# One block of linear attention and a Mish MLP: kv by squares of 64 channels, z in two float32r parts, and a reordered first block

## The chip, the cores and the metric

One core of one Trainium2 chip. The metric is the device time of one execution in microseconds; lower is better. The core has a matmul engine (TensorE, "PE" in the profile; its weight loads are the row "PEld"), VectorE ("DVE"), ScalarE ("ACT"), GpSimd ("POOL") and a queue engine that issues transfers ("SP").

## What is computed

The reference, cut to what matters here. x has 2048 rows of 512 channels; there are 32 heads of 16 channels.

```python
mod = (_silu(c) @ w_mod).reshape(c.shape[0], 6, 1, -1)
sa, ca, ga, sb, cb, gb = (mod[:, i] for i in range(6))

h = _layernorm(x) * (1 + ca) + sa
q, k, v = split_heads(h @ wqkv)                       # 32 heads of 16 channels
phi = lambda t: jnp.where(t > 0, t + 1, jnp.exp(t)) + 1e-6
pq, pk = phi(q), phi(k)
kv  = jnp.einsum("bhsd,bhse->bhde", pk, v)            # 16 x 16 per head
z   = jnp.einsum("bhsd->bhd", pk)
num = jnp.einsum("bhqd,bhde->bhqe", pq, kv)
den = jnp.einsum("bhqd,bhd->bhq", pq, z)[..., None] + 1e-6
x = x + ga * ((num / den) merged @ wo)

h = _layernorm(x) * (1 + cb) + sb
x = x + gb * (mish(h @ w1 + b1) @ w2)                 # 512 -> 1792 -> 512
```

## The kernel before

**Precision.** PE multiplies fp32 operands in two instructions per matmul. Most products instead use operands split in two float32r parts, a high part `h` (a rounding copy) and a low part `l` (the rest), and three matmuls `h*h + h*l + l*h`: that is `mm3` (lines 67 to 69), and `split` (lines 71 to 81) makes the parts, with the copy at L75 (ACT) or L77 (another engine) and the subtraction at L80. A few small products stay in plain fp32: the sums z (L277), their spreading zbc (L476), kv (L738), the products of kv and wo (L748) and the denominators (L591).

**Order.** The kernel is written under a manual schedule: on each engine, instructions run in the order in which the Python code issues them. Work that should lie between PE's units is written as generators; `spawn` adds one, and each `tick` lets every running generator issue its next piece. So moving a line moves its instructions in the queue of its engine. SBUF holds a pool of 101 tiles of 128 x 512, and PSUM has four accumulators ("acc"), three "h" banks and one "tp" bank.

**Stages.** The 2048 rows are four blocks of four tiles of 128 rows.

1. First block (lines 345 to 447). The statistics of the four tiles of x are taken, and `apply` (L339) normalises them, on ACT (L195, which needs a shift computed on DVE, L190) or on DVE (L197). `mod_col` (L162) makes the columns of the modulation: column 0 (shift) and column 4 (scale) are needed first; `plus_one` (L166) adds one. PE transposes the tiles (L371) into `tp0[k]`; ACT writes `hT_x_0_k` as its high half `hi`, and then the full value back in place (both L393); DVE subtracts for the low half (L405). PE then runs the k projections in rounds over the four tiles: high by high (L412), then high by low and low by high (L415).
2. For blocks 0 to 3: `k_unit`, phi of k, and `g_unit`, which adds products of phi(k) with the normalised x to `gacc`. `make_constants` (L140) fills the masks on POOL between the second and the third unit of block 0; right behind it POOL makes the high halves of block 1 (`transpose(..., pool)`, L455), which DVE (L80) and PE need.
3. `z_unit` (L273) sums phi(k) over the rows by four matmuls into four strips of 32 partitions, and ACT copies the result to `zsum`. `z_side` (L473) multiplies it by `w32`, a matrix of 1/32, which adds up the strips on all partitions; ACT copies it to `zbc_sb`, and DVE makes from it the scaled head masks (`hmask`) and `zs`.
4. The q projections (`q_unit`). Between them: `attend` (L586) makes the denominators `den` with stationary operands of 32 columns, four strips side by side (L591); kv is made of 16 matmuls, group g of 128 channels by k (L738), of which only the 16 x 16 squares of the heads are kept by a product with `bmask` (L740); and `m_ps` (L748) multiplies kv by the scaled wo.
5. `o_unit`, the second normalisation, and the MLP by two-by-two blocks with seven products each (`product`, `pair_unit`, `d_unit`).

These are the lines of kv that the change replaces:

```python
    kv_ps = ps("acc", "kv_ps")
    for g in range(4):
        cs = slice(P * g, P * (g + 1))
        for k in range(4):
            pe.matmul(kv_ps[:, cs], wv[k][:, cs], zs[k][:, cs], start=k == 0, stop=k == 3)
```

Of the kernel before, what the change touches and what calls it, by code (L numbers as in the profile page):

```python
# [8 lines left out]
F32 = mybir.dt.float32  # L9
F32R = mybir.dt.float32r  # L10
AF = mybir.ActivationFunctionType
ALU = mybir.AluOpType

P = 128
# [11 lines left out]
def block_kernel(ctx: ExitStack, tc: tile.TileContext, x, wqkv, wo, w1, b1t, w2, c, wmodt, out):  # L26
    nc = tc.nc
    act, dve, pool, pe, sp = nc.scalar, nc.vector, nc.gpsimd, nc.tensor, nc.sync

    cst = ctx.enter_context(tc.tile_pool(name="cst", bufs=1))  # L30
# [7 lines left out]
    def sb(name, dt=F32, shape=(P, 512)):  # L38

        return big.tile(list(shape), dt, tag="T", name=name, bufs=SLOTS)  # L40

    def ps(tag, name, shape=(P, 512)):
        return psp.tile(list(shape), F32, tag=tag, name=name, bufs=PBUFS[tag])

    def f32(t):
        return t.bitcast(F32)
# [14 lines left out]
    def run(gen):  # L61
        for _ in gen:
            pass
# [7 lines left out]
    def split(name, t, keep, key, lo_engine=dve, hi_engine=act):  # L71

        hi, lo = sb(f"{name}h", F32R, t.shape), sb(f"{name}l", F32R, t.shape)
        if hi_engine is act:
            act.activation(hi, t, AF.Copy)  # L75
        else:
            hi_engine.tensor_copy(hi, t)  # L77
        if lo_engine is dve:
            yield
        lo_engine.tensor_tensor(lo, t, f32(hi), op=ALU.subtract)  # L80
        keep[key] = hi, lo


    xt, wm, wraw = {}, {}, {}
# [46 lines left out]
    sc_bc = ps("acc", "sc_bc")  # L131
# [1 line left out]
    warm_up(3)  # L133
    ident = cst.tile([P, P], F32, name="ident")
    make_identity(nc, ident)
    w32 = cst.tile([P, P], F32, name="w32")
    bmask = cst.tile([P, P], F32, name="bmask")
    hmask = cst.tile([P, 4, 32], F32, name="hmask")

    def make_constants():  # L140
        pool.memset(w32, 1.0 / 32)

        pool.memset(bmask, 1.0)
        bm3 = bmask.rearrange("p (a r) -> p a r", r=16)
        pool.affine_select(bm3, bm3, pattern=[[-16, 8], [0, 16]], compare_op=ALU.is_ge,
                           fill=0.0, base=0, channel_multiplier=1)
        pool.affine_select(bm3, bm3, pattern=[[16, 8], [0, 16]], compare_op=ALU.is_ge,
                           fill=0.0, base=15, channel_multiplier=-1)

        pool.memset(hmask, 1.0)  # L150
        pool.affine_select(hmask, hmask, pattern=[[128, 4], [-16, 32]], compare_op=ALU.is_ge,
                           fill=0.0, base=0, channel_multiplier=1)
        pool.affine_select(hmask, hmask, pattern=[[-128, 4], [16, 32]], compare_op=ALU.is_ge,
                           fill=0.0, base=15, channel_multiplier=-1)


    mc = cst.tile([P, 24], F32, name="mc")
    sc_row = sb("sc_row")

    def mod_col(i, row):  # L160
        t = wm.pop(i)
        dve.scalar_tensor_tensor(t, t, 1.0, row, op0=ALU.mult, op1=ALU.mult,  # L162
                                 accum_out=mc[:, i:i + 1])

    def plus_one(lo, hi):
        dve.tensor_scalar(mc[:, lo:hi], mc[:, lo:hi], 1.0, 1.0, op0=ALU.add, op1=ALU.mult)  # L166
# [16 lines left out]
    def ln_rstd(key, b, lo=0, hi=4):  # L183

        y = rs[key, b][:, lo:hi]
        pool.tensor_tensor(y, y, half[:, lo:hi], op=ALU.pow)  # L186

    def ln_shift(key, b, lo=0, hi=4):

        dve.scalar_tensor_tensor(nb[key, b][:, lo:hi], mv[key, b][:, lo:hi, 0], -1.0, rs[key, b][:, lo:hi],  # L190
                                 op0=ALU.mult, op1=ALU.mult)

    def ln_apply(key, b, j, t, dst, engine):
        if engine is act:
            act.activation(dst, t, AF.Identity, bias=nb[key, b][:, j:j + 1], scale=rs[key, b][:, j:j + 1])  # L195
        else:
            engine.tensor_scalar(dst, t, mv[key, b][:, j, 0:1], rs[key, b][:, j:j + 1],  # L197
                                 op0=ALU.subtract, op1=ALU.mult)
# [16 lines left out]
    def sums_shift(key, b, t, sums):  # L215
        dve.tensor_tensor(nb[key, b][:, t:t + 1], sums[:, 0:1], rs[key, b][:, t:t + 1], op=ALU.mult)  # L216

    xn, hT, wq, wk = {}, {}, {}, {}
# [49 lines left out]
            cs = slice(P * k, P * (k + 1))  # L268
            mm3(gacc[k], [h[:, cs] for h in xn[b, t]], pk[b, t], b == 0 and t == 0, b == NB - 1 and t == 3)

    zsum = sb("zsum")

    def z_unit():  # L273

        p = ps("h", "z")
        for t in range(4):
            pe.matmul(p[32 * t:32 * (t + 1), :], ones[:, 0:32], ku.pop((0, t)), start=True, stop=True)  # L277
        act.activation(zsum, p, AF.Copy)

    def q_unit(b, g):  # L280
        p = ps("h", f"pq_{b}_{g}")
# [57 lines left out]
    def apply(b, t, engine, shift=True):  # L339
        v = xt["x", b, t]  # L340
        if engine is act and shift:
            ln_shift("x", b, t, t + 1)
        ln_apply("x", b, t, v, v, engine)

    tp0 = [ps("acc", f"tp_x_0_{k}") for k in range(3)]
# [5 lines left out]
    sums_eps("x", 0, 2, sums)  # L351
    ln_eps("x", 0, 3, 4)
    ln_rstd("x", 0, 3, 4)
    wk_0 = split("wk_0", wraw[1, 0], wk, 0)
    next(wk_0)
    apply(0, 1, dve)
    sums_shift("x", 0, 2, sums)
    apply(0, 2, act, shift=False)
    mod_col(4, sc_bc)
    plus_one(4, 5)  # L360
    apply(0, 3, dve)
    mod_col(0, sc_bc)
    run(wk_0)

    def transposes_0(k, p):
        for t in range(4):
            pe.transpose(p[:, P * t:P * (t + 1)], xt["x", 0, t][:, P * k:P * (k + 1)], ident)
# [6 lines left out]
    def mod_pair(k):  # L374
        mod_col(4 + k, sc_bc)
        plus_one(4 + k, 5 + k)
        mod_col(k, sc_bc)
# [6 lines left out]
    def step(*gens):  # L384
        for g in gens:
            next(g, None)

    tss = [slice(P * t, P * (t + 1)) for t in range(4)]
    for k in range(4):
        hi, lo = sb(f"hT_x_0_{k}h", F32R), sb(f"hT_x_0_{k}l", F32R)  # L390
        hT["x", 0, k] = hi, lo
        for dst in (hi, tp0[k]):
            act.activation(dst, tp0[k], AF.Identity, bias=mc[:, k:k + 1], scale=mc[:, 4 + k:5 + k])  # L393
        if k < 3:
            run(split(f"wk_{k + 1}", wraw[1, k + 1], wk, k + 1, pool, pool))
        if k == 0:
            act.preload_act_table_set("exp_and_others")
            mod_pair(1)
        if k == 1:
            step(xsplit[0])  # L400
            mod_col(7, sc_bc)
            plus_one(7, 8)
        if k == 3:
            step(xsplit[0])
        dve.tensor_tensor(lo, tp0[k], f32(hi), op=ALU.subtract)  # L405
        if k == 0:
            mod_pair(2)
        if k == 1:
            mod_col(3, sc_bc)
        if k < 2:  # L410
            for t in range(4):
                pe.matmul(kp[t], hi[:, tss[t]], wk[k][0], start=k == 0, stop=False)  # L412
            for st, mv_ in (hi, wk[k][1]), (lo, wk[k][0]):
                for t in range(4):
                    pe.matmul(kp[t], st[:, tss[t]], mv_, start=False, stop=False)  # L415
        if k == 0:
            tp0.append(ps("acc", "tp_x_0_3"))
            transposes_0(3, tp0[3])
# [27 lines left out]
    apply(1, 3, act, shift=False)  # L446
    step(xsplit[3], kpost[3])
    make_constants()
    for j in range(4):
        load_x(2, j)  # L450
# [11 lines left out]
    wv, wos = {}, {}  # L462
# [8 lines left out]
    zs = {}  # L471

    def z_side():  # L473

        zbc_ps = ps("tp", "zbc")
        pe.matmul(zbc_ps, w32, zsum, start=True, stop=True)  # L476
        zbc = sb("zbc_sb")
        act.activation(zbc, zbc_ps, AF.Copy)
        yield
        for g in range(4):  # L480
            diag = cst.tile([P, P], F32, tag="diag", name=f"diag_{g}", bufs=1)
            dve.scalar_tensor_tensor(diag, zbc[:, P * g:P * (g + 1)], 1.0, ident, op0=ALU.mult, op1=ALU.mult,
                                     accum_out=zc[:, g:g + 1])
            dve.tensor_scalar(hmask[:, g, :], hmask[:, g, :], zc[:, g:g + 1], 1.0, op0=ALU.mult, op1=ALU.mult)
        for k in range(4):
            zs[k] = sb(f"zs_{k}")
            dve.tensor_scalar(zs[k], zbc, mc[:, k:k + 1], 1.0, op0=ALU.mult, op1=ALU.mult)
# [245 lines left out]
    spawn(attending)  # L733
    kv_ps = ps("acc", "kv_ps")
    for g in range(4):
        cs = slice(P * g, P * (g + 1))
        for k in range(4):
            pe.matmul(kv_ps[:, cs], wv[k][:, cs], zs[k][:, cs], start=k == 0, stop=k == 3)  # L738
    kv = sb("kv")
    dve.tensor_tensor(kv.rearrange("p (g m) -> p g m", g=4), kv_ps.rearrange("p (g m) -> p g m", g=4),  # L740
                      bmask.unsqueeze(1).to_broadcast([P, 4, P]), op=ALU.mult)
    for g in range(1, 4):
        q_unit(1, g)
        load_x(2, g, "r")
# [230 lines left out]
```

## Time and profile before

| what | us |
|---|---|
| median of 3 runs (506.63 to 507.06) | 506.66 |
| the profiled execution | 506.48 |
| its span | 504.8 |
| PE busy | 497.4 |
| DVE busy | 359.7 |
| ACT busy | 256.7 |
| POOL busy | 113.0 |

The span runs from the first to the last instruction of the profile; the 1.7 us between span and time lie around it. "Busy" is the time in which an engine had an instruction under way. Matmuls are pipelined, so a row's duration is longer than its distance from the next: a float32r matmul of 512 columns has a row of 0.39 us, and the next begins 0.23 us later. The chain of waits gives each instruction its share of the time instead, and is the view to take costs of PE from. In the timelines a row reads: start and duration in us, engine, line, operation, output and inputs, shapes, count, and in brackets how long the engine had been idle and what released it.

### The profile page before, as it was taken

The numbers are of one execution on the slowest core, as the hardware profiler recorded it, in microseconds if no ns is written. First come the engines' busy times: TensorE is split into PE (matmuls) and PEld (weight loads), VectorE is DVE, ScalarE is ACT, GpSimd is POOL, SyncE is SP. The second block draws the span as 40 slices with busy tenths as digits, with TensorE's granted clock in tenths as the row PEclk, the third lists the DMA queues.
The fourth block names the chain that finished last, engine by engine and source line by source line (L and its number), as shares of the span: only waits on it lengthen the run. The fifth ranks groups of instructions, "written<-read, shape, count | busy, mean of one in ns | idle before, by whom it ended". The sixth has DMA issues, their size and how long they took to land.

```text
span 504.8 us, 6832 instructions
## 1 busy us (share of the span) xinstructions
PE 497.4 (99%) x2364; PEld 407.8 (81%) x2364; DVE 359.7 (71%) x705; ACT 256.7 (51%) x461; POOL 113.0 (22%) x203
## 2 busy tenths in 40 slices
PE   7999999999999999999999999999999999999996
PEld 6778888878778888878888888888888888888885
DVE  6889785878997969986987785359886556745302
ACT  6767573523351987736677765357253344445000
POOL 4480000100212411210233345421210111470000
PEclk9999999999999999999999999999999999999999
DMA  8721504561543315372566599983842445596102
GB/s 311 274 83 44 166 21 126 167 209 49 139 132 92 88 36 178 104 227 66 156 199 186 144 295 264 347 237 92 242 135 63 125 126 163 137 354 223 41 0 83
DMA packets 52232, 77.28 MB, mean 153 GB/s; under 512 B 5805, under 2 KB 20277, under 8 KB 52198
## 3 DMA queue, kind: packets, MB, share of 16 engines
q0 software_dynamic: 19600, 37.45, 25.6%
q1 hardware_dynamic: 32452, 39.14, 24.8%
q8 instruction: 18, 0.29, 0.2%
q10 hardware_dynamic: 146, 0.26, 0.1%
q14 instruction: 16, 0.13, 0.1%
HBM read 60.83 MB, written 15.99 MB: 152 GB/s over the span
## 4 chain that ended last, share of the span: by engine, by line
PE 88%; DVE 7%; DMA 2%; ACT 1%; POOL 1%; issue 0%; SPq 0%; DVEq 0%; ACTq 0%
PE oacc L68 10%; PE oacc L69 10%; PE oacc L67 10%; PE p_s L67 5%; PE p_s L69 5%; PE p_s L68 5%; PE p_a L68 3%; PE p_a L69 3%; PE p_a L67 3%; PE pq L67 3%; PE pq L68 3%; PE pq L69 3%; PE gacc L68 3%; PE gacc L69 3%; PE gacc L67 3%; PE pk L69 2%
## 5 line engine op out<-in xcount | busy, mean ns | idle before, releaser
L509 POOL DMA_DIRECT2D w2b<-w2d x84 | 44.9, 538 | 102.6 <-PE p_a L69 27.3
L817 ACT ACTIVATE ub<-c,b1c 128x512 f32<-128x512 f32 x28 | 19.1, 719 | 57.2 <-DVE c L826 53.5
L826 DVE TENSOR_TENSOR u<-p_s,u 128x512 f32<-128x512 f32 x28 | 19.3, 691 | 35.2 <-PE p_s L69 25.5
L809 DVE TENSOR_TENSOR rb<-oacc,rb 128x512 f32<-128x512 f32 x8 | 5.5, 692 | 32.9 <-PE oacc L69 32.9
L826 DVE TENSOR_TENSOR u<-p_a,u 128x512 f32<-128x512 f32 x26 | 17.6, 688 | 7.5 <-PE p_a L69 6.9
L691 ACT ACTIVATE hf_n<-tp_n,mc 128x512 f32<-128x512 f32 x16 | 11.7, 772 | 21.1 <-PE tp_n L689 21.1
L186 POOL TENSOR_TENSOR rs_n<-rs_n,half 128x1 f32<-128x1 f32 x16 | 9.4, 589 | 54.1 <-DVE rs_n L212 44.4
L238 ACT ACTIVATE e_q<-pq 128x512 f32<-128x512 f32 x16 | 9.4, 589 | 21.5 <-PE pq L69 21.5
L794 ACT ACTIVATE u<-u,b1c 128x512 f32<-128x512 f32 x26 | 18.5, 713 | 2.6 <-DVE u L826 2.6
L826 DVE TENSOR_TENSOR c<-p_s,u 128x512 f32<-128x512 f32 x28 | 17.9, 683 | 1.9 <-PE p_s L69 1.9
L843 ACT ACTIVATE u<-p_a 128x512 f32<-128x512 f32 x12 | 7.1, 588 | 18.7 <-PE p_a L69 18.7
L238 ACT ACTIVATE e_k<-pk 128x512 f32<-128x512 f32 x16 | 9.4, 591 | 13.4 <-PE pk L69 13.3
L186 POOL TENSOR_TENSOR rs_x<-rs_x,half 128x1 f32<-128x1 f32 (+1 forms) x10 | 7.1, 718 | 32.9 <-DVE rs_x L181 32.1
L240 DVE TENSOR_SCALAR e_k<-e_k 128x512 f32<-128x512 f32 x16 | 6.8, 423 | 10.4 <-ACT e_k L238 10.2
L195 ACT ACTIVATE x<-x,nb_x,rs_x 128x512 f32<-128x512 f32 x14 | 10.8, 806 | 4.3 <-DVE nb_x L190 3.3
L598 POOL DMA_DIRECT2D rden_d<-rden x3 | 2.2, 739 | 47.9 <-DVE rden L596 47.9
L610 DVE TENSOR_TENSOR q<-q,rd 128x512 f32<-128x512 f32 x16 | 10.5, 686 | 2.6 <-DMA rd<-rden_d 2.6
L622 DVE TENSOR_TENSOR r<-o,r 128x512 f32<-128x512 f32 x16 | 10.8, 681 | 1.7 <-PE o L69 1.6
L195 ACT ACTIVATE r<-r,nb_n,rs_n 128x512 f32<-128x512 f32 x8 | 6.5, 808 | 10.1 <-DVE nb_n L216 9.3
L241 DVE SCALAR_TENSOR_TENSOR ku<-pk,e_k 128x512 f32<-128x512 f32 x16 | 11.1, 692 | 0.8
L241 DVE SCALAR_TENSOR_TENSOR q<-pq,e_q 128x512 f32<-128x512 f32 x16 | 11.1, 691 | 0.8
L177 DVE BATCH_NORM_STATS2 st_x<-x 128x6 f32<-128x512 f32 x13 | 8.9, 682 | 3.1 <-DMA x<-in_x_dram 3.1
(1116 smaller groups left out, 1757.0 us busy)
## 6 DMA issues: line engine op xcount, KB each, us to landing
w2b<-w2d POOLq DMA_DIRECT2D x84, 256.0 KB, 4.9
w1p<-in_w_dram SPq DMA_DIRECT2D x28, 256.0 KB, 3.1
wm<-in_wmodt_dram SPq DMA_DIRECT2D x24, 256.0 KB, 5.1
r<-in_x_dram SPq DMA_DIRECT2D x16, 256.0 KB, 2.6
x<-in_x_dram SPq DMA_DIRECT2D x15, 256.0 KB, 5.3
w2r<-in_w_dram SPq DMA_DIRECT2D x14, 256.0 KB, 3.4
rd<-rden_d POOLq DMA_DIRECT2D x12, 256.0 KB, 5.3
wr<-in_wqkv_dram SPq DMA_DIRECT2D x8, 256.0 KB, 3.0
```

The lines of the kernel that those rows point to most:

```text
L67: pe.matmul(o, st[0], mv[0], start=start, stop=False)
L68: pe.matmul(o, st[0], mv[1], start=False, stop=False)
L69: pe.matmul(o, st[1], mv[0], start=False, stop=stop)
L186: pool.tensor_tensor(y, y, half[:, lo:hi], op=ALU.pow)
L195: act.activation(dst, t, AF.Identity, bias=nb[key, b][:, j:j + 1], scale=rs[key, b][:, j:j + 1])
L238: act.activation(e, p, AF.Exp)
L241: dve.scalar_tensor_tensor(dst, p, 0.0, e, op0=ALU.max, op1=ALU.add)
L509: pool.dma_start(w2s[f][i], w2d[f, i])
L691: act.activation(hf[b, j], p, AF.Identity, bias=mc[:, 12 + j:13 + j], scale=mc[:, 16 + j:17 + j])
L794: act.activation(u, p, AF.Mish, bias=b1c[:, f:f + 1])
L817: act.activation(u, p, AF.Mish, bias=b1c[:, f:f + 1])
L826: dve.tensor_tensor(out, p, u, op=ALU.add)
```

## The change

- `z_unit` keeps the sums as two float32r parts, `zsum[0]` (copied by ACT) and `zsum[1]` (the rest, subtracted by DVE); `z_side` multiplies `w32`, now float32r as well, by both in turn.
- kv is made by squares of 64 by 64 channels: in each group of 128, two matmuls, one to PSUM partitions 0 to 63 and one to 64 to 127, with 64 stationary and 64 moving columns each. Two masked copies on 64 partitions replace the one on 128. What they leave out of the kv tile is zeroed beforehand: the tile is taken at the start and POOL zeroes it in `make_constants`.
- In the first block ACT, not DVE, normalises tile 1. The column products 4 and their `plus_one` come before the shift of tile 2, and the split of the first k weights, `wk_0`, comes behind column 0, in one go.
- The high half of `hT_x_0_0` is written by ACT in two pieces of 256 columns.

```diff
-    w32 = cst.tile([P, P], F32, name="w32")
+    w32 = cst.tile([P, P], F32R, name="w32")
...
+    kv = sb("kv")
+
     def make_constants():
-        pool.memset(w32, 1.0 / 32)
+        pool.memset(f32(w32), 1.0 / 32)
+        pool.memset(kv, 0.0)
...
-    zsum = sb("zsum")
+    zsum = [sb(f"zsum_{i}", F32R) for i in range(2)]
...
-        act.activation(zsum, p, AF.Copy)
+        act.activation(zsum[0], p, AF.Copy)
+        dve.tensor_tensor(zsum[1], p, f32(zsum[0]), op=ALU.subtract)
...
-    wk_0 = split("wk_0", wraw[1, 0], wk, 0)
-    next(wk_0)
-    apply(0, 1, dve)
+    apply(0, 1, act)
+    mod_col(4, sc_bc)
+    plus_one(4, 5)
     sums_shift("x", 0, 2, sums)
     apply(0, 2, act, shift=False)
-    mod_col(4, sc_bc)
-    plus_one(4, 5)
     apply(0, 3, dve)
     mod_col(0, sc_bc)
+    wk_0 = split("wk_0", wraw[1, 0], wk, 0)
     run(wk_0)
...
-        for dst in (hi, tp0[k]):
-            act.activation(dst, tp0[k], AF.Identity, bias=mc[:, k:k + 1], scale=mc[:, 4 + k:5 + k])
+
+        for dst, piece in [(hi, half_) for half_ in ((0, 256), (256, 512))] + [(tp0[k], (0, 512))] if k == 0 else \
+                [(hi, (0, 512)), (tp0[k], (0, 512))]:
+            cs = slice(*piece)
+            act.activation(dst[:, cs], tp0[k][:, cs], AF.Identity, bias=mc[:, k:k + 1], scale=mc[:, 4 + k:5 + k])
...
-        pe.matmul(zbc_ps, w32, zsum, start=True, stop=True)
+        for i in range(2):
+            pe.matmul(zbc_ps, w32, zsum[i], start=i == 0, stop=i == 1)
...
     for g in range(4):
-        cs = slice(P * g, P * (g + 1))
         for k in range(4):
-            pe.matmul(kv_ps[:, cs], wv[k][:, cs], zs[k][:, cs], start=k == 0, stop=k == 3)
-    kv = sb("kv")
-    dve.tensor_tensor(kv.rearrange("p (g m) -> p g m", g=4), kv_ps.rearrange("p (g m) -> p g m", g=4),
-                      bmask.unsqueeze(1).to_broadcast([P, 4, P]), op=ALU.mult)
+            for j in range(2):
+                cs = slice(P * g + 64 * j, P * g + 64 * (j + 1))
+                pe.matmul(kv_ps[64 * j:64 * (j + 1), cs], wv[k][:, cs], zs[k][:, cs], start=k == 0, stop=k == 3)
+    for j in range(2):
+        js = slice(64 * j, 64 * (j + 1))
+        dve.tensor_tensor(kv.rearrange("p (g m) -> p g m", g=4)[js, :, js],
+                          kv_ps.rearrange("p (g m) -> p g m", g=4)[js, :, js],
+                          bmask[js, js].unsqueeze(1).to_broadcast([64, 4, 64]), op=ALU.mult)
```

## The prediction

> **What bounds the kernel now.** I read the page first, then the list of what TensorE (PE) waited for, then the chain of waits in order of time, and last the timelines of the engines around each edit. The page says who is busy and who ends the chain:
>
> ```profile
> PE 497.4 (99%) x2364; PEld 407.8 (81%) x2364; DVE 359.7 (71%) x705; ACT 256.7 (51%) x461; POOL 113.0 (22%) x203
> ...
> PE 88%; DVE 7%; DMA 2%; ACT 1%; POOL 1%; issue 0%; SPq 0%; DVEq 0%; ACTq 0%
> ```
>
> PE is busy for 99% of the span, and 88% of the chain that ended last lies on it. The list of PE's own waits is the second half of that statement:
>
> ```profile
> PE pk L412 <- ACT hT_x_0h L393: 0.7, 1, 0.7
> ...
> PE gacc L68 <- DVE rs_x L212: 0.2, 1, 0.2
> ```
>
> The first is the largest wait for data that an edit here touches, and the rows between and after it are shorter ones. After the first block PE simply works through its instructions in order. So a microsecond less of PE work, anywhere behind the first block, should come off the end, unless another engine then becomes late; and a microsecond of delay on DVE, ACT or POOL costs nothing until it reaches PE. The chain in order of time shows the PE stretches that the change shortens (start, length in us, what):
>
> ```profile
> 107.14 0.86 PE zbc L476 x2
> 108.00 0.23 PE pq L67
> ...
> 121.64 1.01 PE den L591 x32
> 122.65 3.77 PE kv_ps L738 x32
> 126.42 0.24 PE pq L67
> ...
> 143.65 1.01 PE den L591 x32
> 144.66 0.43 PE pq L67
> ```
>
> Each fp32 matmul is two rows: 16 kv matmuls give x32, one zbc matmul x2. A float32r matmul of the same 512 columns is one row of 0.23 us, where the fp32 one takes 0.86.
>
> **The change, part by part.**
>
> *z in two parts.* One fp32 matmul (0.86) becomes two float32r ones over the same 512 columns: 2 x 0.23 = 0.46. That removes 0.40 us of PE. What it adds is a subtraction on DVE, which must follow the copy on ACT:
>
> ```profile
> 104.31 0.60 ACT L278 ACTIVATE zsum<-z 128x512 f32<-128x512 f32 x1 [3.20 <-PE z L277]
> ```
>
> DVE's next wait in this stretch, and the nearest row to the new subtraction (also fp32, 128x512, one operand from PSUM), are
>
> ```profile
> 108.67 0.29 DVE L482 SCALAR_TENSOR_TENSOR diag<-zbc_sb,ident 128x128 f32<-128x128 f32 x1 [2.52 <-ACT zbc_sb L478]
> ...
> 126.46 0.69 DVE L740 TENSOR_TENSOR kv<-kv_ps,bmask 128x512 f32<-128x512 f32 x1 [1.34 <-PE kv_ps L738]
> ```
>
> The subtraction can begin at 104.31 + 0.60 = 104.91 and, at 0.69, ends near 105.65; PE asks for it at 107.14, so 1.5 us of last-half-block matmuls cover it. While it waits for ACT it holds up what stands behind it in DVE's order: two scalings of wo and the low halves wq_2l and wq_3l. These four take about 2.8 us at 0.69 each and then end near 108.4. The first q unit, from 107.6 on, reads a low half only in every third matmul, wq_2l in its 9th (109.4) and wq_3l in its 12th (110.1): nobody waits. DVE sat idle for 2.52 us before the diagonal, so its extra work is paid from idle time. If that cover were gone, the price would be at most one 0.69. I take -0.40.
>
> *kv by squares.* The 16 matmuls of 128 columns by 128 become 32 of 64 by 64, each pair in the two column halves of the array, so x32 rows become x64. No row of before has this shape. The nearest is den: 32 stationary columns, four column strips side by side, 128 moving columns, and 32 rows in 1.01 us. That is 31.6 ns per row, against 3.77 / 32 = 118 ns for kv: the four strips do overlap, nearly four times over. A pair of squares needs half of kv's 118 ns and two run together, so the array time per row is 118 / 2 / 2 = 29 ns, close to the rate that den reached. At den's rate 64 rows take 2.02 us. Bounds: 1.9 us by array time, and 64 x 59 = 3.77 us if the pairs do not overlap at all. I take 2.02, since den is the same mechanism at the same rate of instructions.
> A rule of the Trainium skill speaks against pieces this small: "TensorE: Matmul & The Clock Gate", section "Wait — 56ns, not 53.3ns?", says that with decoding in firmware the sequencer spends about 62 ns on each matmul, which binds once the array's work is shorter. By it the 64 would take 4.0 us and this part would be +0.4, not -1.5. The den rows, at 31.6 ns, are half of that, so it does not seem to hold here.
> Leaving the tiled shape also costs: the first whole-array row behind den takes 0.43 us where others take 0.23, and behind kv it now takes 0.24. Since kv becomes tiled too, its successor should pay this 0.19 (the switch from den into kv exists already). Part: 2.02 + 0.19 - 3.77 = -1.56; with something for the switch between strips of 32 and of 64, I take -1.5.
>
> The copy behind kv (the DVE row at 126.46) goes from one masked product to two on half the partitions and half the columns. Two can cost at most 2 x 0.69 = 1.4 us, starting about 1.5 earlier on a DVE that waited 1.34 for it. They end before 126.5. The matmuls that read kv come only after three more q units, of twelve 0.23 rows each, some 8 us later. Zero cost.
>
> *The zeroing of kv* goes to POOL, into the constants, ahead of work that PE needs soon. POOL's rows:
>
> ```profile
> 0.80 0.10 POOL L118 MEMSET half<- 128x4 f32 x1 [0.29 <-POOLq L964]
> ...
> 32.17 0.20 POOL L141 MEMSET w<- 128x128 f32 x1
> ...
> 34.42 0.61 POOL L77 CAST hT_x_0h<-hf_x 128x512 fp32r<-128x512 f32 x1
> ```
>
> 4 columns take 0.10 and 128 take 0.20, so 512 should take about 0.5 us (an estimate along that line). Behind it on POOL stand the other masks and then the four casts that give block 1 its high halves, and DVE's subtractions wait for those. The one with least to spare is the third:
>
> ```profile
> 37.07 1.09 DVE L80 TENSOR_TENSOR hT_x_2l<-hf_x,hT_x_2h 128x512 fp32r<-128x512 f32 x1
> ```
>
> ```profile
> 38.54 0.39 PE L69 MATMUL pk<-wk_2h,hT_x_2l 128*128 128x512 f32 x1
> ```
>
> It ends at 38.16 and PE uses it at 38.54: 0.38 us of cover against 0.5 of delay. A stall of 0.12, and some restart of PE, make +0.2. Bounds: 0 if the memset hides in a slow select of the mask, +0.6 if it is itself slowed by DVE as much as that subtraction is (1.09 against 0.69: 0.5 becomes 0.8, less 0.38, with restart).
>
> *First block.* These rows carry it:
>
> ```profile
> 7.62 0.54 DVE L197 TENSOR_SCALAR x<-x,mv_x,rs_x 128x512 f32<-128x512 f32 x1
> ...
> 8.31 0.69 DVE L162 SCALAR_TENSOR_TENSOR wm<-wm,sc_bc 128x512 f32<-128x512 f32 x1
> 8.54 0.80 ACT L195 ACTIVATE x<-x,nb_x,rs_x 128x512 f32<-128x512 f32 x1
> ...
> 10.35 0.78 ACT L393 ACTIVATE hT_x_0h<-tp_x,mc 128x512 fp32r<-128x512 f32 x1 [1.02 <-PE tp_x L371]
> ...
> 11.18 1.20 PE L412 MATMUL pk<-wk_0h,hT_x_0h 128*128 128x512 f32 x4 [0.70 <-ACT hT_x_0h L393]
> ...
> 12.18 0.69 DVE L405 TENSOR_TENSOR hT_x_0l<-tp_x,hT_x_0h 128x512 fp32r<-128x512 f32 x1
> ...
> 13.13 1.09 PE L415 MATMUL pk<-wk_0h,hT_x_0l 128*128 128x512 f32 x4
> ```
>
> Tile 1 moves from DVE to ACT, and the high half of the first weights, that ACT did there, moves behind tile 2. On DVE the first column product (0.69) and two small steps take the place of tile 1 (0.54) ahead of the shift of tile 2. ACT can begin tile 2 only when that shift is there, which I estimate 0.2 later, at 8.75 in place of 8.54; so the last transposes and the start of hT_x_0h come 0.2 later, at 10.55. In return only its first half must be done before PE starts. How much shorter a half is, ACT shows elsewhere:
>
> ```profile
> 135.15 0.62 ACT L75 ACTIVATE a_1h<-w1p 128x512 fp32r<-128x512 f32 x1
> ...
> 137.35 0.40 ACT L75 ACTIVATE a_1h<-w1p 128x256 fp32r<-128x256 f32 x1
> ```
>
> 0.22 us. So the two cancel, and PE starts near 11.2 as before. Behind it ACT is later by 0.2 (the start) and 0.2 (one more instruction, less the overlap), so tp_x is ready near 12.25; DVE, which would take it at 12.18, takes it at about 12.3, and the third round of PE at 13.13 slips by 0.1. If instead the first half could begin before the last transposes, PE would start earlier and meet that third round anyway, which needs hT_x_0l at 12.18 + 0.69 = 12.87: no more than 0.26 to win. I take +0.1, from -0.26 to +0.4 (ACT's whole delay reaching PE).
>
> **The sum:** -0.40 - 1.5 + 0.2 + 0.1 = -1.6 us. The profiled execution took 506.48 us (span 504.8), which is 0.18 under the median of 506.66; so 504.9 against its own time, and 505.1 against the median. What a measurement of this kernel can tell from no change is about 0.2%, 1.0 us.
>
> **The rivals.**
>
> *The pairs do not overlap.* If two squares share what only one can use, a row costs 59 ns and kv stays at 3.77 us; with the switch and the other parts, +0.19 - 0.40 + 0.3 = +0.1: 506.8 us. For it: no row of before has two strips of 64, and 64 columns loaded per strip are twice den's. Against: den's four strips at 31.6 ns. The Trainium skill's 62 ns per matmul, from the page named above, would end 0.2 higher still. 10%.
>
> *Each pair drains before the next.* If a strip's weights could be replaced only when both matmuls have ended, a round would cost a whole lone matmul. The PE row at 38.54 lasts 0.39 us for 512 columns that stream in 0.23; 64 columns stream in 0.03, so a lone square lasts about 0.19, 32 rounds 6.1 us, 2.3 more than kv now: with the +0.1 of the rival before it, 509.1 us, slower. It decides from 0.146 us per round on: (3.77 + 1.0 - 0.1) / 32. Den replaces its weights in every round too and shows nothing of it. 5%.
>
> *The small delays are larger.* First block and memset at their upper ends: +0.4 + 0.6 in place of +0.3, so 505.8. For it: both places have less than 0.4 us of cover. 10%.
>
> **How the numbers follow.** The forecast, 505.1, has 75%; its own range, 504.4 to 505.6, is from kv at array time and the first block at its best to kv 0.3 worse and a memset stall of 0.4. The third rival (10%) ends at 505.8, which is within 0.2% of before; the first (10%) at 506.8 also; the second (5%) is slower. The range 504.3 to 506.1 holds forecast and third rival. Faster by over 0.2% (under 505.65): 0.78, the forecast with some of the third rival; same: 0.16; slower: 0.06.
>
> **What the changed profile would show.** kv_ps as x64, 64 columns wide, and from the last den row to the next q unit about 2.2 us in the chain, not 3.8; about 3.8 there means the first rival. zbc as two rows of 0.23, and the subtraction of zsum on DVE with an idle time before it, released by ACT. A POOL memset of about 0.5 near 32.3, hT_x_2l later by as much, and a PE wait of 0.1 to 0.3 near 38.5. The first row of L412's successor near 11.2, its first two matmuls ahead of the second piece. Behind 140 us every stretch the same length, 1.6 us earlier: if they are not, a DVE or DMA wait near a stage's start has taken the gain, and the forecast is wrong in its first step, that PE alone sets the end.

## The result, and the profile after

| | before | after |
|---|---|---|
| median, us | 507.42 | 505.63 |
| lowest to highest of 17 runs each | 506.45 to 508.88 | 504.80 to 507.87 |
| profiled execution (span) | 506.48 (504.8) | 506.47 (504.7) |

The ratio of the times is 0.9967, with a 95% interval of 0.9955 to 0.9979: the changed kernel is faster, by 0.33%. In the other sets of runs, below, the kernel before had medians of 506.76 to 506.91, so its 507.42 here is on the high side. The two profiled executions, however, are equally long: after's was 0.84 us above its own median, before's 0.94 below its own. The runs of both kernels are spread over 2.4 to 3.1 us, more than the change is worth, and the profile of after shows one way in which a run gets long. So it is read here for two things: whether PE's work became shorter, and where that was lost again.

The first part of the page, and the shares of the chain that ended last, of after:

```profile
PE 495.5 (98%) x2396; PEld 404.9 (80%) x2396; DVE 360.3 (71%) x707; ACT 257.8 (51%) x463; POOL 112.9 (22%) x204
...
PE 84%; DVE 9%; DMA 4%; issue 1%; ACT 1%; POOL 1%; DVEq 0%; POOLq 0%; ACTq 0%
```

PE is busy for 1.9 us less than before (497.4), and the span is the same. The chain runs over PE for 84% instead of 88%, and over DVE and DMA for 13% instead of 9%.

**The edits.** The chain of after shows zbc, and the chain of the kernel without the first block's edits (below) shows kv with its neighbours (start, length, what):

```profile
107.34 0.46 PE zbc L483 x2
```

```profile
121.29 1.01 PE den L596 x32
122.30 2.02 PE kv_ps L744 x64
124.32 0.42 PE pq L67
```

zbc has 0.46 in place of 0.86, kv 2.02 in place of 3.77, and the row behind kv pays 0.18 more than before for leaving the tiled shape. The timeline of POOL in after, then that of DVE, then that of PE, show the memset and what it pushes:

```profile
32.43 0.52 POOL L144 MEMSET kv<- 128x512 f32 x1
...
34.77 0.61 POOL L77 CAST hT_x_0h<-hf_x 128x512 fp32r<-128x512 f32 x1
```

```profile
37.42 1.09 DVE L80 TENSOR_TENSOR hT_x_2l<-hf_x,hT_x_2h 128x512 fp32r<-128x512 f32 x1
```

```profile
38.68 0.40 PE L69 MATMUL pk<-wk_2h,hT_x_2l 128*128 128x512 f32 x1
```

The memset takes 0.52, the casts start 0.35 later than before (0.12 of it was there ahead of the memset: the memset of `w32` began at 32.29 in place of 32.17), and PE's matmul with hT_x_2l follows the one ahead of it after 0.23 us: no wait. The first block, from the timelines of DVE and PE:

```profile
4.36 0.69 DVE L180 BATCH_NORM_STATS2 st_x<-x 128x6 f32<-128x512 f32 x1 [2.90 <-DMA x<-in_x_dram]
```

```profile
10.97 1.20 PE L418 MATMUL pk<-wk_0h,hT_x_0h 128*128 128x512 f32 x4 [0.44 <-ACT hT_x_0h L399]
...
14.40 0.94 PE L418 MATMUL pk<-wk_1h,hT_x_1h 128*128 128x512 f32 x3
```

x happened to land 0.17 us earlier than in the profile of before (4.36 against 4.53). PE starts 0.21 earlier and has lost that by its second high-by-high round (14.40 against 14.41): against the landing of x it is 0.16 later. The other profiles bear this out: from the landing of x to the first product of gacc it takes 18.37 to 18.43 us in the six profiles with the first block's edits, and 18.17 in before. Without the edits the order is not always that quick: five of those eight profiles have 18.15 to 18.22, the other three 18.44 to 18.90.

**Where PE's lead went.** The table sets the start of the same matmul in two profiles side by side; negative means earlier than in before. "p_s" is the first product that reads b_2h; "rd" is the median time from issue to landing of the four transfers of rd for the first attend; the last two columns are all runs. Each profile is one execution. The kernel before was run again beside each group of four kernels, in the order of the table from kv_alone on, with medians of 506.76, 506.91 and 506.83, and each ratio is to the runs of its own group.

| kernel | m_ps (134.45) | o, qs_2l (151.98) | p_s (220.74) | end | rd, us | median (lowest to highest) | ratio to before, 95% |
|---|---|---|---|---|---|---|---|
| before | 0 | 0 | 0 | 0 | 5.9 | see above | |
| after | -1.77 | -0.73 | -0.02 | -0.04 | 9.2 | 505.63 (504.80 to 507.87) | 0.9967 (0.9955 to 0.9979) |
| kv_alone | -1.17 | -0.53 | +1.08 | +1.04 | 8.6 | 506.83 (505.04 to 508.10) | 1.0004 (0.9993 to 1.0015) |
| z_alone | -0.28 | -0.28 | -0.26 | -0.31 | 5.2 | 506.13 (505.96 to 506.40) | 0.9986 (0.9978 to 0.9995) |
| first_alone | +0.26 | +0.26 | +0.27 | +0.24 | 6.2 | 506.72 (506.62 to 507.51) | 0.9996 (0.9985 to 1.0008) |
| kv_and_z | -1.90 | -1.89 | -1.23 | -1.27 | 7.8 | 504.97 (504.49 to 505.76) | 0.9967 (0.9956 to 0.9979) |
| after_wm13_held | -1.65 | -1.65 | -1.65 | -1.68 | 5.8 | 504.77 (504.63 to 504.84) | 0.9946 (0.9927 to 0.9965) |
| before_wm13_free | +0.06 | +0.95 | +3.60 | +3.56 | 9.2 | 509.77 (507.61 to 511.49) | 1.0038 (1.0018 to 1.0057) |
| after_r_first | -1.87 | -0.62 | -0.89 | -0.87 | 9.1 | 505.49 (504.58 to 507.27) | 0.9962 (0.9946 to 0.9979) |
| before_r_first | +0.02 | +0.02 | -0.42 | -0.45 | 7.6 | 506.23 (505.74 to 507.37) | 0.9981 (0.9965 to 0.9997) |
| kv_wm13_held | -1.44 | -1.44 | -1.41 | -1.40 | 4.8 | 505.11 (504.96 to 505.60) | 0.9962 (0.9949 to 0.9975) |
| serial_wm13_held | -0.26 | -0.26 | -0.25 | -0.30 | 5.0 | 506.48 (506.18 to 506.70) | 0.9987 (0.9979 to 0.9996) |
| held_r_first | -1.65 | -1.65 | -2.09 | -2.13 | 4.9 | 504.36 (503.95 to 504.48) | 0.9945 (0.9931 to 0.9959) |
| kvz_held_r_first | -1.20 | -1.20 | -1.19 | -1.24 | 5.3 | 504.80 (504.66 to 505.24) | 0.9956 (0.9943 to 0.9969) |

In after the lead of 1.77 us at m_ps falls to 0.73 at 152 us and to nothing at 221 us. The list of PE's waits names two places; neither wait was in before's list:

```profile
PE p_s L67 <- DVE r L629: 0.7, 1, 0.7
...
PE o L69 <- DVE qs_2l L80: 0.4, 1, 0.4
```

Both times PE waits for DVE. A third wait is too short for that list: PE's row at 145.98, which needs q from DVE, begins 0.53 us after the row ahead of it in place of 0.23. Matmul by matmul against before, the lead falls by 0.42 us there, by 0.73 at 151.25 and by 0.58 at 219.23. DVE's timeline, before first and then after, says what made it late (the bracket is the idle time ahead of the row and its releaser):

```profile
139.91 1.28 DVE L610 TENSOR_TENSOR q<-q,rd 128x512 f32<-128x512 f32 x2
141.70 0.69 DVE L80 TENSOR_TENSOR m_0l<-m_ps,m_0h 128x512 fp32r<-128x512 f32 x1 [0.51 <-ACT m_0h L75]
```

```profile
140.68 0.69 DVE L617 TENSOR_TENSOR q<-q,rd 128x512 f32<-128x512 f32 x1 [2.12 <-DMA rd<-rden_d]
141.71 0.69 DVE L617 TENSOR_TENSOR q<-q,rd 128x512 f32<-128x512 f32 x1 [0.34 <-DMA rd<-rden_d]
142.32 0.68 DVE L80 TENSOR_TENSOR m_0l<-m_ps,m_0h 128x512 fp32r<-128x512 f32 x1
```

Before, DVE multiplied q by rd without a wait and then waited for m_ps, that is for PE. After, it waits 2.12 + 0.34 us for the transfer of rd, and the low part of m comes 0.62 us later than before, although PE made m_ps 1.77 earlier. The transfers themselves, seen in the landing times of that attend, before and after:

```profile
DMA to landing us min/median/max: 5.2/5.9/6.6
```

```profile
DMA to landing us min/median/max: 8.0/9.2/10.4
```

They carry the same 256 KB each; what differs is SP's queue beside them. Before, with the wait that holds its third load, and then after:

```profile
133.06 0.33 SPq L93 DMA_DIRECT2D wm<-in_wmodt_dram  x1
133.48 0.38 SPq L89 DMA_DIRECT2D r<-in_x_dram  x1
138.08 0.33 SPq L93 DMA_DIRECT2D wm<-in_wmodt_dram  x1
138.50 0.38 SPq L89 DMA_DIRECT2D r<-in_x_dram  x1
```

```profile
SPq L93 <- PE m_ps L748: 4.1, 1, 4.1
```

```profile
131.29 0.33 SPq L93 DMA_DIRECT2D wm<-in_wmodt_dram  x1
131.71 0.38 SPq L89 DMA_DIRECT2D r<-in_x_dram  x1
132.19 0.38 SPq L93 DMA_DIRECT2D wm<-in_wmodt_dram  x1
132.66 0.38 SPq L89 DMA_DIRECT2D r<-in_x_dram  x1
```

rd is issued from 134.1 us in before and from 132.7 in after. Before, two loads go out ahead of it and the second pair waits until m_ps has ended (138.08). After, all four go out ahead of it. The reason is where the second load, wm_13, goes. Tiles of the pool are handed out again in the order in which they come free. In before, wm_13 got the tile of kv, which m_ps reads last, and so it held up SP's queue until then. In after kv sits in a tile taken at the start, the order has shifted, and wm_13 gets the tile of e_q_1_1, which is free by then: the wait for m_ps is gone from SP's list.

The second place is older than the change. The chain of before, from 182 to 219 us, is not on PE at all:

```profile
182.89 2.55 DMA rden_d<-rden
185.59 0.62 SPq L602
186.31 4.37 DMA rd<-rden_d
190.75 0.57 issue
191.32 0.69 DVE b_0l L80
...
218.60 0.61 DVE r L622
219.25 0.50 PE p_s L67
```

Denominators of the last attend, their two transfers, and then 28 us, in which DVE is busy for 27 (the chain passes over ACT for 4.4), lead to the sum r<-o,r that frees a PSUM bank for PE. PE reached this place 0.3 us ahead of DVE already in before: the matmul ahead of 219.25 began at 218.72, 0.53 earlier in place of 0.23. In after the chain enters by a later one of the four transfers, 8.04 us of it, and ends at the same time:

```profile
187.86 8.04 DMA rd<-rden_d
...
218.58 0.61 DVE r L629
...
219.23 0.50 PE p_s L67
```

### The profile page after: what moved, and what is told of

It reads as the page before. It is cut to its first block, busy times and chain, and to the rows that moved or that the text cites. A ratio compares the mean times of both kernels' runs of the same rounds, so it can differ in the third digit from the quotient of the medians.

```text
span 504.7 us, 6900 instructions
## 1 busy us (share of the span) xinstructions
PE 495.5 (98%) x2396; PEld 404.9 (80%) x2396; DVE 360.3 (71%) x707; ACT 257.8 (51%) x463; POOL 112.9 (22%) x204
## 4 chain that ended last, share of the span: by engine, by line
PE 84%; DVE 9%; DMA 4%; issue 1%; ACT 1%; POOL 1%; DVEq 0%; POOLq 0%; ACTq 0%
PE oacc L69 10%; PE oacc L67 10%; PE oacc L68 10%; PE p_s L67 5%; PE p_s L69 5%; PE p_s L68 5%; PE p_a L67 3%; PE p_a L69 3%; PE p_a L68 3%; DMA rd<-rden_d 3%; PE gacc L68 3%; PE gacc L69 3%; PE gacc L67 3%; PE pk L69 2%; PE pk L68 2%; PE pk L67 2%
```

## The experiments

**One part of the change at a time.** The first three kernels are before with one part of the diff each: the lines of kv with its early tile and memset, the lines of zsum and w32, the lines of the first block. The fourth is after without the first block's edits.

```diff
kv_alone:     + kv = sb("kv") at the start, pool.memset(kv, 0.0), squares of 64
z_alone:      + zsum in two float32r parts, w32 float32r
first_alone:  + apply(0, 1, act), mod_col(4) first, wk_0 in one go, hT_x_0_0h in two pieces
kv_and_z:     + the first two together
```

> The kernel before with kv by squares and the zeroing of the kv tile alone. Theory A (PE sets the end, kv's saving is real): the trace of the changed kernel has kv at 2.02 us in place of 3.59 to 3.77 and its successor's gap 0.34; with 0 to 0.2 for the memset the end moves by -1.3 to -1.6 us, ratio 0.9968 to 0.9975. Theory B (the saving is made and given back at the first DMA it meets): since kv's tile is taken early here too, wm_13's load takes a tile that is free early, wm_12, r, wm_13 and r lie beside the transfer of rd, rd lands late, DVE's product of q with rd waits about 2 us, and PE is ahead of before by 1.5 us at 143 us but only by 0.2 to 0.5 at 156 us: -0.2 to -0.8 us, ratio 0.9984 to 0.9996.

> The kernel before with z in two float32r parts alone. All theories: zbc is 2 x 0.23 us in place of 0.86, DVE's subtraction is covered, and PE is 0.4 us earlier at 143 us. Theory A: all of it reaches the end, -0.4 us, ratio 0.9992, which is near what 5 rounds can tell. Theory B: the same here, because the loads of wm_12 and wm_13 should still wait for m_ps (they take tiles that m_ps frees), so rd lands as in before.

> The kernel before with the first block's new order and the two pieces of hT_x_0_0h alone. The prediction's sum: +0.1 us (from -0.26 to +0.4). From the trace of the changed kernel, where x landed 0.17 earlier and PE's second k unit still started no earlier: +0.2 to +0.35 us, ratio 1.0004 to 1.0007. If the order helps (theory of the change): PE starts 0.2 earlier and block 1's first pk starts 0.2 earlier than 36.73 us, ratio below 0.9997.

> All of the change but the first block's order and pieces. Theory A (parts add): 0.3 us below the whole change if the first block costs 0.2 to 0.35, so a ratio to before of 0.996 where the whole change has 0.9967. Theory B: PE is ahead by 1.9 us at 143 us and by only 0.7 to 0.9 at 156 us, since rd lands as late as in the changed kernel; ratio 0.9962 to 0.998. If the first block costs nothing the ratio equals that of the whole change, 0.9967.

kv alone gave nothing that can be measured: 1.0004, above the range of theory B, whose upper part (to 0.9996) its interval just reaches. Its trace has what B named: kv at 2.02 us, four loads ahead of rd, rd at 8.6 us, PE's lead of 1.17 at m_ps down to 0.53 at 152 us; and it goes on to be 1.08 behind at 221 us, which B had not said; that execution was a long one, 507.51 against a median of 506.83. z alone gave 0.9986, with 0.9992 inside its interval, and it is the kernel with the smallest spread of the four, 0.44 us: here m_ps still frees the tile of wm_13. First alone is 0.9996: neither +0.1 nor +0.3 nor a small gain can be told from nothing by it. Kv and z together match the whole change. In this profile the lead lived past 152 us although rd took 7.8 us and DVE waited 1.4 for it; 0.65 was then lost at 217 us to r<-o,r. So kv's part is there on PE, and what reaches the end differs from run to run.

**Who holds the loads.** One line, which only chooses the tile of one load:

```diff
 def load_wmod(i):
-    wm[i] = sb(f"wm_{i}")
after_wm13_held:   + wm[i] = wos[3] if i == 13 else sb(f"wm_{i}")
before_wm13_free:  + wm[i] = zs[3] if i == 13 else sb(f"wm_{i}")
```

> The changed kernel with one load's destination changed: wm_13 goes into the tile of wo_3, which m_ps reads last, so that SP's queue waits there for the end of m_ps (near 136.2 us), as it does in the kernel before (138.05). Theory C (part of the gain is lost because the tile that wm_13 gets has changed and four loads now lie beside rd): rd lands before 139.2 us, DVE does not wait for it, PE's lead over before is still 1.7 us at 156 us and above 1.2 us at 219 us, the end is 0.4 to 1.0 us below the changed kernel's, ratio to before 0.9948 to 0.9960, and the runs scatter by about 1 us, not 3. Rival D (rd's transfers scatter by themselves, and these loads have nothing to do with it): ratio 0.9967 and a scatter of 3 us, as the changed kernel.

> The kernel before with one load's destination changed: wm_13 goes into the tile of zs_3, which kv reads last (126.4 us), so that nothing holds SP's queue and the loads of wm_13 and the r behind it go out near 134 us, beside rd. Theory C: rd lands 1 to 3 us later than 139.9 us, DVE waits for it, and the end is 0.3 to 1.2 us later, ratio 1.0006 to 1.0024, with a wider scatter than the kernel before. Rival D: no difference, ratio 0.9995 to 1.0005.

SP's queue in the first of the two; wm_13 is now the row that writes wo:

```profile
131.41 0.33 SPq L93 DMA_DIRECT2D wm<-in_wmodt_dram  x1
131.83 0.38 SPq L89 DMA_DIRECT2D r<-in_x_dram  x1
136.43 0.33 SPq L93 DMA_DIRECT2D wo<-in_wmodt_dram  x1
136.85 0.38 SPq L89 DMA_DIRECT2D r<-in_x_dram  x1
```

```profile
140.05 0.69 DVE L80 TENSOR_TENSOR m_0l<-m_ps,m_0h 128x512 fp32r<-128x512 f32 x1 [0.18 <-ACT m_0h L75]
```

rd lands in 5.8 us, DVE waits for m_ps again, and 1.65 us of lead stay to the end. Eight runs lie within 0.21 us. Theory C holds: held, the change is worth 0.9946, and its median is close to the fastest run of the kernel as it was changed (504.80). The other direction was as clear and larger than expected: before with wm_13 set free is 1.0038, its runs lie over 3.9 us, and rd needs 9.2 us. The list of PE's waits in it:

```profile
PE p_s L67 <- DVE r L622: 1.1, 1, 1.1
...
PE o L67 <- DVE c L826: 1.1, 1, 1.1
```

I had expected +0.3 to +1.2 us; DVE became so late that PE also waited at a third place, c<-p_a,u. Rival D, that the loads have nothing to do with it, falls in both directions. The line changes which tiles some later transfers get as well, but the two edits point opposite ways and each moved the time the way in which it moved the loads. How the loads make rd late shows in part in the records of the transfers' packets. rd comes in 256 packets of 4 KB. The first of them starts 1.42 to 1.64 us after rd's first issue in the nine profiles with two loads ahead, and 2.15 to 2.78 us after it in the five with four. After that the packets themselves were slow in after, a mean of 0.36 us each against 0.26 in before; but in before_r_first they took 0.41, and SP's queue moved next to nothing from 136 to 141 us. So the late start goes with the loads, and what slows the packets stays open.

**The order of r on DVE.**

```diff
     for t in (2, 3):
         o_unit(NB - 1, t, "h")
+        running.insert(0, fresh.pop())
         tick()
```

> The changed kernel with another order on DVE near 216 us: the two sums r<-o,r of the last two o units are issued ahead of the other generators of their tick, not behind them. No work is taken away. PE's first product of pair_unit waits there for r (0.73 us of idle, a gap of 1.11 in place of 0.23). Theory E (from 183 us on, DVE and the transfer of rd set the end, so that PE's lead is lost at 219 us): the gap falls below 0.5, PE's lead at 219 us is as large as at 180 us, and the end is 0.5 to 0.9 us earlier than the changed kernel's: ratio to before 0.9949 to 0.9957. Rival F (PE sets the end, that wait is one of many): another wait takes its place, ratio 0.9967.

> The kernel before with the same order on DVE. The gap there is 0.53 in place of 0.23 (after a pause, of which about 0.1 is the start): theory E gives 0.2 to 0.3 us here, ratio 0.9994 to 0.9996, much less than in the changed kernel, since before PE and DVE reach this place almost together. Rival F: no difference in either, ratio 1.000. If the gain here were as large as in the changed kernel (0.9982), the lead of PE has nothing to do with it.

In both traces PE's wait for r is gone. In after the lead grows there, from 0.45 us at 216 us to 0.89; the loss at 152 us stays. The time, 0.9962 against 0.9967 of the unchanged order, says nothing: the runs lie over 2.7 us. In before the trace gains 0.44 us and the time 0.9981, where I had expected 0.2 to 0.3 us and the smaller gain of the two. So the place is real and DVE sets it, but the claim that it costs much more after the change than before is not shown. Part of the miss in size: PE's pause costs more than its length, for the row after it is 0.34 us from its successor in place of 0.23 (219.25 and 219.59).

**The same questions without the spread.** With wm_13 held, differences of half a microsecond can be read. The label of the fourth kernel names the order of r, which it does not have.

```diff
kv_wm13_held:      kv_alone with the line of after_wm13_held
serial_wm13_held:  after_wm13_held, with
-    for g in range(4):
-        for k in range(4):
-            for j in range(2):
+    for j in range(2):
+        for g in range(4):
+            for k in range(4):
held_r_first:      after_wm13_held with the order of r
kvz_held_r_first:  after_wm13_held without the first block's edits
```

> The run of kv by squares alone, with wm_13's load into wo_3's tile as in after_wm13_held. Theory C: kv alone gave nothing (1.0004) only because its tile, taken early, moved the four loads beside rd; with the load held again, PE's 1.55 us stay: -1.2 to -1.6 us, ratio 0.9966 to 0.9976, scatter of about 1 us. Rival D: kv by squares is worth nothing at the end for another reason (its copies on DVE, POOL's memset): ratio 1.000 again.

> after_wm13_held with all squares of the lower half first, then all of the upper half, so that the two squares of a pair no longer follow each other; the same 32 matmuls, the same weights. Theory of the prediction (the two halves of the array work at the same time): a row costs 59 ns alone, kv takes 3.6 to 3.8 us in place of 2.02, PE loses 1.6 to 1.8 us, ratio to before 0.9978 to 0.9984. Rival G (it is the smaller matmul alone that is cheap, with no overlap): kv stays at 2.02 us and the ratio at 0.9946. Rival H (each lone square also drains): 64 x 95 ns or more, over 6 us, ratio above 1.002.

> The whole change with both repairs: wm_13's load held, and r<-o,r first in its tick. After_wm13_held still had a gap of 0.54 at 217.06 us in place of 0.23. Theory E: the gap closes, 0.3 us below after_wm13_held: 504.4 to 504.6 us where before has 506.4 to 506.9, ratio 0.9940 to 0.9958. If DVE no longer matters once rd lands early: as after_wm13_held.

> The whole change but the first block, with wm_13's load held, without the order of r. Against after_wm13_held it gives the price of the first block's order in a kernel without scatter: by the traces so far (PE's lead 1.65 with it, 1.90 without it) 0.1 to 0.25 us less, ratio to before 0.994; if the first block helps, more by 0.1 to 0.3 us.

Kv alone goes from 1.0004 to 0.9962 by the tile of one load, a little more than expected: the part that seemed worthless is the largest. With the pairs taken apart, the chain of serial_wm13_held shows

```profile
122.25 3.70 PE kv_ps L746 x64
```

57.8 ns per row against 31.6 in pairs: the overlap is shown, and rivals G and H fall. The ratio, 0.9987, lies just above the expected 0.9978 to 0.9984, nearly all of which is in its interval (0.9979 to 0.9996). The order of r on top of the held load gives the fastest kernel here, 504.36, 0.4 us below after_wm13_held (of another set of runs) in time as in the trace (2.13 against 1.68 at the end), and PE waits for r no more. Without the first block's edits the time is 504.80 against 504.77 with them (of another set of runs), intervals 0.9943 to 0.9969 and 0.9927 to 0.9965: its price was not found. In that profile the first k weights landed late (ACT waited 0.99 us for `wr`, in before 0.25), PE started 0.61 us later than in before, and so its lead is no evidence either.

## Why the prediction was right, and where it was not

The forecast was 505.1 us and -0.31% of the median; measured were 505.63 and -0.33%. The median is 0.03 above the forecast's own range, 504.4 to 505.6, and inside the wider one that takes in the third rival. The sum was sound, and its agreement with the time is partly chance, because one step failed.

*z in two parts, -0.40.* As forecast: zbc takes 0.46. The subtraction ran at 105.14 behind ACT's copy and ended before PE asked; zbc began at 107.34, and DVE still waited (0.23 us) before the diagonal.

*Kv by squares, -1.5.* 2.02 us for 64 rows, the value taken from den's rate, and 0.18 of the 0.19 for the switch. From the q units ahead (108 us) to m_ps, PE gains 1.55 to 1.58 us in every profile that has the pairs. The first rival, no overlap, is what serial_wm13_held brings about, at 3.70 us; the second, a drain in every round, did not show even there. (Its lone square was priced with the 0.03 us that 64 columns take in float32r; at the 59 ns of an fp32 row a round would cost 0.22 us, not 0.19. Nothing hung on that.) The Trainium skill's page "TensorE: Matmul & The Clock Gate", section "Wait — 56ns, not 53.3ns?", with 62 ns per matmul for decoding in firmware, does not bind here if a row counts as a matmul: rows started every 31.6 ns on average. The prediction's 4.0 us rests on that count. With a matmul of the program, which is two rows, the page's figure gives an estimate of 32 x 62 ns = 2.0 us, the forecast's own value, so kv does not decide against it; den does by a little, with 110 ns for each round of four rows, 55 ns per matmul of the program. "TensorEngine Tiling (Array Packing)", section "Theoretical Speedup", gives up to twice the speed for 64 columns; the trace has 3.70 / 2.02 = 1.83. Both times hold some 0.15 us at the two ends, and in serial_wm13_held a few rows still overlap where the strips change; between the ends a pair of rows starts every 58 ns, as a lone row does in serial_wm13_held, so there the factor is 2.

*The zeroing, +0.2.* It cost PE nothing that the trace shows: 0.52 us as estimated, but only 0.23 of it reached the casts, since a select of the mask behind it took 0.35 us in place of 0.57. That was the lower bound. But the step had costed only the memset. Taking kv's tile at the start was part of the same edit, and it is this that moved wm_13.

*The first block, +0.1.* In the trace 0.16 later against the landing of x at the second high-by-high round, and 0.19 to 0.26 later at the first product of gacc in the six profiles that have it; the measured ratio does not resolve it.

*The first step, that behind the first block PE alone sets the end.* It failed, in the way that the prediction had named as its test: a DMA wait near a stage's start took the gain. The lines shown with it had the warning in them: 9% of the chain was DVE and DMA. I read 88% as "PE" and did not ask where the 9% lay. It lies in two stretches, the first 30 us and the 36 us from 183 to 219, and in the second the kernel before was already waiting for a transfer and then for DVE. A gain on PE passes there only if DVE's start moves as well, and that start hangs on the landing of rd. But only 0.58 us were lost in that stretch. The other 1.15 went at 146 and 151 us, where the chain of before lies on PE; they came from the moved load, of which the 9% say nothing.

*Why the sum agrees with the time nevertheless.* after_wm13_held, where nothing is given back, is at 504.77, 1.5 to 1.7 us below the fastest runs of before (506.3 to 506.5): that is the sum of -1.6. Medians are another matter: the runs of before reach 2.4 us above their fastest, those of after 3.1. For after the early loads explain that, since with wm_13 held the spread is 0.21; what lengthens some runs of before, whose loads are held, stays open, and the 1.8 us between the two medians hold that as well. The third rival, with its 505.8, was near the measured time and wrong in its cause: neither the first block nor the memset was what gave time back.

## What to carry to other kernels

A large share of PE in the chain is no licence for the rest: take the few per cent that lie elsewhere, find the stretches in which they lie, and ask of a gain ahead of them whether it gets through. When tiles are handed out in order of release, an edit that takes one tile earlier or later also changes which work every later load waits for; compare the start times of the loads before and after, not only the computation. And when the runs of a kernel lie further apart than the change is worth, look for the transfer that decides them first: here one tile made runs within 0.21 us of runs within 3, and made half-microsecond questions answerable.

## What the runs showed of the hardware

- Four transfers of 256 KB, issued on POOL's queue, landed in a median of 4.8 to 6.2 us where two other loads of 256 KB had been issued on SP's queue within 2 us ahead of the first of them, and in 7.8 to 9.2 us where four were issued within 2 us ahead of it or 0.6 us behind it. One profile of the first kind, before_r_first, had 7.6, with slow packets and nothing beside them (above); so the loads are not all that delays rd. The page "DMA: Bandwidth & Descriptors" of the Trainium skill, section "Issuing engines are not separate DMA queues", says that transfers run on the same engines and interleave whoever issued them; the later start of rd's packets with four loads ahead fits that, though how the engines shared the two queues was not looked at.
- fp32 rows in column strips started every 31.6 ns on average, in strips of 32 columns with 128 moving (den) and in strips of 64 with 64 moving (kv), but not evenly: the two rows of a kv pair start 7 ns apart and the pairs 58 ns apart; the four rows of a den round start within 20 ns and the rounds 110 ns apart. Rows alone start every 58 ns with 64 moving columns (serial_wm13_held) and every 112 ns with 128 (kv in before). So strips overlap in full, and the average is higher only by the ends of the stretch.
- POOL's first select of a 128 x 128 mask took 0.57 us in the five profiles without the memset of kv and 0.35 in the nine with it, without an edit to it.
